# Attention and GEGLU FFN on one core: a hand-written interleaved order, values as stationary operand, and q and k turned by transposing DMAs

## The chip, the core and the metric

The kernel runs on one NeuronCore of a Trainium2 chip. The metric is the device time of one execution in microseconds (us). The core has five engines that work side by side, each with its own instruction queue: TensorE (PE; its weight loads are listed apart as PEld), VectorE (DVE), ScalarE (ACT), GpSimd (POOL) and SyncE (SP). Instructions of one engine are issued in the order of its queue. Transfers run on DMA engines; POOL and SP issue them.

## What is computed

Eight batches with eight heads go through causal attention with a window of 128 positions and a distance bias; the result feeds a gated FFN.

```python
# q, k, v: [8, 8, 576, 64]
scores = scale * q @ k.T                                   # scale = 1/8
rel = pos[:, None] - pos[None, :]
mask = (rel >= 0) & (rel < 128)
scores = where(mask, scores - slope[h] * abs(rel), -1e9)   # slope[h] = 2**-(h+1)
attn = exp(scores - max); attn = attn / (sum(attn) + 1e-9)
x = (attn @ v) -> [4608 tokens, 512]
out = (gelu(x @ w_gate) * (x @ w_val)) @ w_out             # 512 -> 1536 -> 512
```

## The kernel before

Data is bf16 on chip, sums are float32 in PSUM. A batch has 576 positions, that is five tiles of 128 keys (the last of 64). Work is written as two functions, `attention_bp` for a pair of batches and `ffn_group` for 512 tokens, called in the order: pair 0, groups 0 and 1, pair 1, groups 2 and 3, pair 2, groups 4 and 5, pair 3, groups 6 to 8. No order of the engines' queues is written out; the framework's scheduler places the instructions by their dependences, and pools of buffers limit how far it runs ahead.

*Attention of a pair.* q, k and v are loaded from POOL with a cast to bf16, five DMAs each for a batch (`qsb`, `ksb`, `vsb`; L113, L132). q and k must stand with the head dimension on partitions: TensorE transposes each in four chunks of two heads (five transposes a chunk, L98), and the results are copied out of PSUM by ScalarE and VectorE in turn (`evac`, L90 and L92) into `qT` and `kT`. For each head and key tile, one matmul for each of the two batches gives the scores (L158; the keys are the stationary operand, 64 partitions of head dimension, up to 256 queries are streamed). ScalarE takes the exponent (L164) and VectorE multiplies by the mask with the bias, `emask` (L168). For the product with v the probabilities `pT` are the stationary operand and v with an appended column of ones is streamed (`vp`, 65 columns, L185): nine short matmuls for a batch and head. The 65th column of the result is the row sum. VectorE takes its reciprocal, five values a partition (L192, L193), and multiplies (L195, L201) into `xnat`, which has tokens on partitions. TensorE transposes `xnat` (L98 again) into `xT`, features on partitions, as the FFN needs it.

*FFN group.* For each of 12 slices of the hidden size, four matmuls with `wg` and four with `wv` (L222, L231), 512 tokens each, a gelu on ScalarE (L227), and a product on VectorE into `hT` (L235). Then four token tiles of 12 matmuls with `wo` (L240), copied out in turn by ScalarE and VectorE (L90, L92) and stored by SP (L246).

PSUM is split into pools: three banks for scores and transposes (`sc`), two for value products (`opp`), two for gate and value (`gv`), one for the output (`po`).

Of the kernel before, what the change touches and what calls it, by code (L numbers as in the profile page):

```python
# [10 lines left out]
ALU = mybir.AluOpType  # L12


@with_exitstack
def kernel(
# [10 lines left out]
    nc = tc.nc  # L27
# [5 lines left out]
    NKT = (S + 127) // 128  # L33
    LAST = S - 128 * (NKT - 1)

    consts = ctx.enter_context(tc.tile_pool(name="consts", bufs=1))
    slab_pool = ctx.enter_context(tc.tile_pool(name="slabs", bufs=2))
    qkT_pool = ctx.enter_context(tc.tile_pool(name="qkT", bufs=3))
    v_pool = ctx.enter_context(tc.tile_pool(name="vp", bufs=3))
    pT_pool = ctx.enter_context(tc.tile_pool(name="pT", bufs=3))  # L40
    xnat_pool = ctx.enter_context(tc.tile_pool(name="xnat", bufs=2))
    r_pool = ctx.enter_context(tc.tile_pool(name="rp", bufs=4))
    ffn_sb = ctx.enter_context(tc.tile_pool(name="ffn_sb", bufs=3))
    out_sb_pool = ctx.enter_context(tc.tile_pool(name="out_sb", bufs=3))
    ps_sc = ctx.enter_context(tc.tile_pool(name="ps_sc", bufs=3, space=bass.MemoryType.PSUM))
    ps_o = ctx.enter_context(tc.tile_pool(name="ps_o", bufs=2, space=bass.MemoryType.PSUM))
    ps_gv = ctx.enter_context(tc.tile_pool(name="ps_gv", bufs=2, space=bass.MemoryType.PSUM))
    ps_out = ctx.enter_context(tc.tile_pool(name="ps_out", bufs=1, space=bass.MemoryType.PSUM))

    ident = consts.tile([128, 128], BF16)  # L50
    nc.gpsimd.memset(ident, 0.0)
    nc.gpsimd.affine_select(
        out=ident, in_=ident, compare_op=ALU.not_equal, fill=1.0,
        base=0, pattern=[[-1, 128]], channel_multiplier=1,
    )

    emask = consts.tile([128, H, 256], BF16)
    init_pool = tc.alloc_tile_pool(name="init", bufs=1)
    relt = init_pool.tile([128, 256], mybir.dt.int32)
    tmpl = init_pool.tile([128, 256], FP32)  # L60
    nc.gpsimd.iota(relt, pattern=[[1, 256]], base=0, channel_multiplier=-1)
    nc.gpsimd.tensor_copy(out=tmpl, in_=relt)
    nc.gpsimd.affine_select(
        out=tmpl, in_=tmpl, compare_op=ALU.is_ge, fill=1e9,
        base=0, pattern=[[1, 256]], channel_multiplier=-1,
    )
    nc.gpsimd.affine_select(
        out=tmpl, in_=tmpl, compare_op=ALU.is_ge, fill=1e9,
        base=W - 1, pattern=[[-1, 256]], channel_multiplier=1,
    )  # L70
# [3 lines left out]
    init_pool.release()  # L74

    wg = consts.tile([128, 4, DFF], BF16)
    wv = consts.tile([128, 4, DFF], BF16)
    wo = consts.tile([128, 12, DM], BF16)

    xT = consts.tile([128, 4, NTOK], BF16)  # L80

    qspan = [(128 * j, min(256, S - 128 * j)) for j in range(NKT)]
    pslot = [256 * j for j in range(NKT)]
    PTW = 256 * (NKT - 1) + LAST

    evac_flip = [0]

    def evac(dst, src):
        if evac_flip[0] % 2 == 0:
            nc.scalar.copy(out=dst, in_=src)  # L90
        else:
            nc.vector.tensor_copy(out=dst, in_=src)  # L92
        evac_flip[0] += 1

    def pe_transpose_block(ps_bf16, src):
        for j in range(NKT):
            sz = 128 if j < NKT - 1 else LAST
            nc.tensor.transpose(  # L98
                out=ps_bf16[:, 128 * j:128 * j + sz],
                in_=src(j, sz),  # L100
                identity=ident[0:sz, 0:sz],
            )

    def attention_bp(bp):
        bb = (2 * bp, 2 * bp + 1)
        qT, kT, vnat, xnat = {}, {}, {}, {}
        for b in bb:
            qsb = slab_pool.tile([128, NKT, DM], BF16, name="qsb")
            ksb = slab_pool.tile([128, NKT, DM], BF16, name="ksb")
            for sb, src in ((qsb, q), (ksb, k)):  # L110
                for j in range(NKT):
                    sz = 128 if j < NKT - 1 else LAST
                    nc.gpsimd.dma_start(  # L113
                        out=sb[0:sz, j, :].rearrange("p (h d) -> p h d", h=H),
                        in_=src[b][:, 128 * j:128 * j + sz, :].rearrange(
                            "h p d -> p h d"),
                    )

            qT[b] = qkT_pool.tile([128, 4, S], BF16, name="qT")
            kT[b] = qkT_pool.tile([128, 4, S], BF16, name="kT")  # L120
            for sb, dst in ((qsb, qT[b]), (ksb, kT[b])):
                for c in range(4):
                    pst = ps_sc.tile([128, 512], FP32, name="sc")
                    pstb = pst.bitcast(BF16)
                    pe_transpose_block(
                        pstb, lambda j, sz: sb[0:sz, j, 128 * c:128 * (c + 1)])
                    evac(dst[:, c, :], pstb[:, 0:S])

            vsb = slab_pool.tile([128, NKT, DM], BF16, name="vsb")
            for j in range(NKT):  # L130
                sz = 128 if j < NKT - 1 else LAST
                nc.gpsimd.dma_start(  # L132
                    out=vsb[0:sz, j, :].rearrange("p (h d) -> p h d", h=H),
                    in_=v[b][:, 128 * j:128 * j + sz, :].rearrange(
                        "h p d -> p h d"),
                )
            vnat[b] = v_pool.tile([128, NKT, H, 65], BF16, name="vp")
            nc.vector.memset(vnat[b][:, :, :, 64:65], 1.0)  # L138
            nc.vector.tensor_copy(
                out=vnat[b][:, 0:NKT - 1, :, 0:64],  # L140
                in_=vsb[:, 0:NKT - 1, :].rearrange("p j (h d) -> p j h d", h=H),
            )
            nc.vector.tensor_copy(
                out=vnat[b][0:LAST, NKT - 1, :, 0:64],
                in_=vsb[0:LAST, NKT - 1, :].rearrange("p (h d) -> p h d", h=H),
            )
            xnat[b] = xnat_pool.tile([128, NKT, DM], BF16, name="xnat")

        for h in range(H):
            hc, hp = h // 2, (h % 2) * 64  # L150
            pT = pT_pool.tile([128, 2, PTW], BF16)
            for j in range(NKT):
                kp = 128 if j < NKT - 1 else LAST
                q0, nq = qspan[j]
                sc = ps_sc.tile([128, 512], FP32, name="sc").rearrange(
                    "p (x n) -> p x n", x=2)
                for i, b in enumerate(bb):
                    nc.tensor.matmul(  # L158
                        out=sc[0:kp, i, 0:nq],
                        lhsT=kT[b][hp:hp + 64, hc, 128 * j:128 * j + kp],  # L160
                        rhs=qT[b][hp:hp + 64, hc, q0:q0 + nq],
                        start=True, stop=True,
                    )
                nc.scalar.activation(  # L164
                    out=pT[0:kp, :, pslot[j]:pslot[j] + nq],
                    in_=sc[0:kp, :, 0:nq], func=AF.Exp, scale=0.125,
                )
                nc.vector.tensor_tensor(  # L168
                    out=pT[0:kp, :, pslot[j]:pslot[j] + nq],
                    in0=pT[0:kp, :, pslot[j]:pslot[j] + nq],  # L170
                    in1=emask[0:kp, h:h + 1, 0:nq].to_broadcast((kp, 2, nq)),
                    op=ALU.mult,
                )

            for i, b in enumerate(bb):
                opp = ps_o.tile([128, NKT, 65], FP32, name="opp")
                for qt in range(NKT):
                    qs = 128 if qt < NKT - 1 else LAST
                    mms = []
                    if qt > 0:  # L180
                        mms.append((qt - 1, pslot[qt - 1] + 128))
                    mms.append((qt, pslot[qt]))
                    for mi, (j, col) in enumerate(mms):
                        kp = 128 if j < NKT - 1 else LAST
                        nc.tensor.matmul(  # L185
                            out=opp[0:qs, qt, :],
                            lhsT=pT[0:kp, i, col:col + qs],
                            rhs=vnat[b][0:kp, j, h, :],
                            start=(mi == 0), stop=(mi == len(mms) - 1),
                        )  # L190
                r = r_pool.tile([128, NKT], FP32)
                nc.vector.reciprocal(r[:, 0:NKT - 1], opp[:, 0:NKT - 1, 64])  # L192
                nc.vector.reciprocal(  # L193
                    r[0:LAST, NKT - 1:NKT], opp[0:LAST, NKT - 1, 64:65])
                nc.vector.tensor_tensor(  # L195
                    out=xnat[b][:, 0:NKT - 1, 64 * h:64 * h + 64],
                    in0=opp[:, 0:NKT - 1, 0:64],
# [91 lines left out]
```

## Time and profile before

| what | value |
|---|---|
| median of 3 runs | 528.34 us (527.97 to 529.66) |
| span of the profiled execution, first to last instruction | 527.3 us |
| TensorE busy | 487.2 us, 92% |
| VectorE busy | 205.2 us, 39% |
| ScalarE busy | 188.4 us, 36% |
| POOL busy | 105.7 us, 20% |
| mean granted TensorE clock | 0.880 |

The profiled execution's span lies about 1 us below the median of the runs: the span leaves out what stands ahead of the first and behind the last instruction. In a group's row, the names are output<-input, then the shapes (partitions x elements), the count, the busy time, the mean in ns of one, and the idle time just before such instructions with what ended it. Matmuls are pipelined, so the length of one is longer than the distance between two starts. In a row of stretches, the first numbers are the limits and the length, then the busy time of PE, PEld, DVE, ACT and POOL with counts, the granted clock, the DMA share and GB/s.

### The profile page before, as it was taken

What the parts mean: (1) busy time and instruction counts of PE and PEld (TensorE: products, weight loads), DVE (VectorE), ACT (ScalarE), POOL (GpSimd) and SP (SyncE); (2) the same over time, 40 slices, a digit from 0 to 9 for tenths busy, and PEclk for the clock granted to TensorE, in tenths of its full rate; (3) what the DMA queues carried; (4) which work ended last, traced back from release to release, by engine and by line L of the source; (5) the groups of instructions that cost most, each with busy time, mean ns of one, the idle gap of its engine ahead of it and who ended that gap; (6) DMA issues with size and microseconds to landing.
All of it is one profiled execution on the core that took longest, in us unless ns stands there. A gap on an engine that the chain in (4) does not pass through costs nothing.

```text
span 527.3 us, 6826 instructions
## 1 busy us (share of the span) xinstructions
PE 487.2 (92%) x2638; PEld 239.9 (45%) x2672; DVE 205.2 (39%) x614; ACT 188.4 (36%) x350; POOL 105.7 (20%) x133
## 2 busy tenths in 40 slices
PE   3499899999989899999899999999899899999995
PEld 1255554444555544444555544444455434444432
DVE  0255644333354653142345643232354633232331
ACT  3166243132365243122565152132565232132220
POOL 9961796300440030002720000000000000000000
PEclk9999999999955589999955599999855589999999
DMA  9999999910990070102990000101100000201102
GB/s 88 138 178 210 158 142 101 106 40 2 125 90 1 0 47 0 61 20 31 167 63 2 0 1 1 73 8 41 42 0 1 0 1 0 81 1 41 40 0 81
DMA packets 120336, 28.76 MB, mean 55 GB/s; under 512 B 113136, under 2 KB 114672, under 8 KB 120304
## 3 DMA queue, kind: packets, MB, share of 16 engines
q0 software_dynamic: 115120, 18.88, 47.2%
q1 hardware_dynamic: 5184, 9.44, 4.7%
q8 instruction: 21, 0.34, 0.3%
q14 instruction: 11, 0.09, 0.0%
HBM read 37.75 MB, written 9.44 MB: 89 GB/s over the span
## 4 chain that ended last, share of the span: by engine, by line
PE 80%; DMA 6%; POOL 5%; ACT 4%; DVE 3%; issue 1%; another core or an unknown queue 1%; DVEq 0%; POOLq 0%; ACTq 0%
PE gv L231 20%; PE gv L222 17%; PE po L240 17%; PE opp L185 10%; PE sc L158 8%; PE sc L98 7%; DMA wv<-in_moe_w_val_dram 4%; DMA ksb<-in_k_dram 2%; POOL ksb L113 2%; POOL vsb L132 2%; POOL qsb L113 1%; ACT pT L164 1%; DVE hT L235 1%; ACT L164 1%
## 5 line engine op out<-in xcount | busy, mean ns | idle before, releaser
L235 DVE TENSOR_TENSOR hT<-gv,gelu 128x512 bf16<-128x512 f32 x108 | 74.7, 692 | 116.3 <-PE gv L231 111.9
L222 PE MATMUL gv<-xT,wg 128*128 128x512 bf16 x419 | 112.9, 388 | 2.4 <-ACT gelu L227 2.0
L231 PE MATMUL gv<-xT,wv 128*128 128x512 bf16 x420 | 112.6, 385 | 2.3 <-DVE hT L235 1.0
L227 ACT ACTIVATE gelu<-gv 128x512 bf16<-128x512 f32 x108 | 64.5, 597 | 133.5 <-PE gv L222 124.4
L240 PE MATMUL po<-wo,hT 128*128 128x512 bf16 x423 | 98.5, 379 | 2.7 <-ACT osb L90 1.3
L164 ACT ACTIVATE pT<-sc 128x512 bf16<-128x512 f32 (+2 forms) x160 | 71.2, 513 | 44.0 <-PE sc L158 27.5
L158 PE MATMUL sc<-qT,kT 64*128 64x256 bf16 (+2 forms) x320 | 75.0, 354 | 6.1 <-ACT pT L164 5.2
L185 PE MATMUL opp<-vp,pT 128*128 128x65 bf16 (+2 forms) x576 | 75.6, 246 | 4.3 <-DVE xnat L201 4.1
L231 PEld LDWEIGHTS <-wv 128*128 128x128 bf16 x432 | 42.4, 98 | 65.7 <-issue 27.5
L185 PEld LDWEIGHTS <-pT 128*128 128x128 bf16 (+2 forms) x576 | 46.9, 122 | 42.3 <-issue 11.8
L222 PEld LDWEIGHTS <-wg 128*128 128x128 bf16 x432 | 42.0, 98 | 52.3 <-issue 3.6
L240 PEld LDWEIGHTS <-hT 128*128 128x128 bf16 x432 | 41.8, 98 | 52.0 <-issue 4.0
L168 DVE TENSOR_TENSOR pT<-pT,emask 128x512 bf16<-128x512 bf16 (+2 forms) x160 | 48.5, 359 | 6.1 <-ACT pT L164 5.6
L113 POOL DMA_DIRECT2D qsb<-in_q_dram x40 | 34.4, 897 | 59.3 <-PE sc L98 59.1
L113 POOL DMA_DIRECT2D ksb<-in_k_dram x40 | 33.8, 888 | 54.4 <-PE sc L98 35.7
L92 DVE COPY osb<-po 128x512 f32<-128x512 f32 x18 | 12.5, 692 | 80.4 <-PE po L240 75.1
L132 POOL DMA_DIRECT2D vsb<-in_v_dram x40 | 34.0, 895 | 47.2 <-DVE vp L138 38.6
L158 PEld LDWEIGHTS <-kT 64*128 64x128 bf16 (+1 forms) x320 | 31.2, 122 | 26.0 <-issue 10.2
L192 DVE RECIPROCAL r<-opp 128x4 f32<-128x4 f32 x64 | 10.8, 176 | 61.5 <-PE opp L185 61.0
L90 ACT COPY osb<-po 128x512 f32<-128x512 f32 x18 | 10.5, 585 | 67.5 <-PE po L240 64.5
L98 PE MATMUL sc<-ident,qsb 128*128 128x128 bf16 (+1 forms) x160 | 19.2, 242 | 14.5 <-DMA qsb<-in_q_dram 13.2
L90 ACT COPY xT<-sc 128x576 bf16<-128x576 bf16 x16 | 10.2, 638 | 46.3 <-PE sc L98 46.3
(33 smaller groups left out, 198.4 us busy)
## 6 DMA issues: line engine op xcount, KB each, us to landing
out_dram<-osb SPq DMA_DIRECT2D x36, 256.0 KB, 2.0
qsb<-in_q_dram POOLq DMA_DIRECT2D x32, 128.0 KB, 4.4
ksb<-in_k_dram POOLq DMA_DIRECT2D x32, 128.0 KB, 4.9
vsb<-in_v_dram POOLq DMA_DIRECT2D x32, 128.0 KB, 4.1
wg<-in_moe_w_gate_dram POOLq DMA_DIRECT2D x1, 1536.0 KB, 12.1
wv<-in_moe_w_val_dram POOLq DMA_DIRECT2D x1, 1536.0 KB, 18.7
wo<-in_moe_w_out_dram POOLq DMA_DIRECT2D x1, 1536.0 KB, 25.6
qsb<-in_q_dram POOLq DMA_DIRECT2D x8, 64.0 KB, 4.0
```

The costliest lines, as they stand in the source:

```text
L98: nc.tensor.transpose(out=ps_bf16[:, 128 * j:128 * j + sz], in_=src(j, sz), identity=ident[0:sz, 0:sz],)
L113: nc.gpsimd.dma_start(out=sb[0:sz, j, :].rearrange("p (h d) -> p h d", h=H), in_=src[b][:, 128 * j:128 * j + sz, :].rearrange("h p d -> p ...
L132: nc.gpsimd.dma_start(out=vsb[0:sz, j, :].rearrange("p (h d) -> p h d", h=H), in_=v[b][:, 128 * j:128 * j + sz, :].rearrange("h p d -> p h ...
L158: nc.tensor.matmul(out=sc[0:kp, i, 0:nq], lhsT=kT[b][hp:hp + 64, hc, 128 * j:128 * j + kp], rhs=qT[b][hp:hp + 64, hc, q0:q0 + nq], start=T ...
L164: nc.scalar.activation(out=pT[0:kp, :, pslot[j]:pslot[j] + nq], in_=sc[0:kp, :, 0:nq], func=AF.Exp, scale=0.125,)
L168: nc.vector.tensor_tensor(out=pT[0:kp, :, pslot[j]:pslot[j] + nq], in0=pT[0:kp, :, pslot[j]:pslot[j] + nq], in1=emask[0:kp, h:h + 1, 0:nq] ...
L185: nc.tensor.matmul(out=opp[0:qs, qt, :], lhsT=pT[0:kp, i, col:col + qs], rhs=vnat[b][0:kp, j, h, :], start=(mi == 0), stop=(mi == len(mms) ...
L222: nc.tensor.matmul(out=pg, lhsT=wg[:, c, 128 * f:128 * (f + 1)], rhs=xT[:, c, t0:t0 + 512], start=(c == 0), stop=(c == 3),)
L227: nc.scalar.activation(out=gelu, in_=pg, func=AF.Gelu)
L231: nc.tensor.matmul(out=pv, lhsT=wv[:, c, 128 * f:128 * (f + 1)], rhs=xT[:, c, t0:t0 + 512], start=(c == 0), stop=(c == 3),)
L235: nc.vector.tensor_tensor(out=hT[:, f, :], in0=pv, in1=gelu, op=ALU.mult)
L240: nc.tensor.matmul(out=po, lhsT=hT[:, f, 128 * t:128 * (t + 1)], rhs=wo[:, f, :], start=(f == 0), stop=(f == 11),)
```

## The change

The kernel is rewritten with a manual order: on each engine the instructions stand as the program writes them. The unit is now one batch b and one FFN group g = b - 1. Batch 0 is done first, alone. Then for each group: its 12 gate/value slices, and after them the attention of batch g + 1 with the group's output matmuls, cut into eight halves of six matmuls (`out_half`), set between its parts. Groups 7 and 8 have no attention beside them.

- A chunk c is two heads. Scores of its two heads are issued alternately (i = 0, 1; partitions 0 to 63 and 64 to 127) into two banks. Key tiles are shifted by 64 positions, so that tile 0 holds 64 zero keys and 64 real ones, and queries are streamed 192, 256, 256, 256 and 128 at a time. Masks are applied to both heads at once, 1024 and 1152 elements a partition (`emask`, and `emask2`, a second arrangement of it).
- In `values`, v (64 columns of a head) is the stationary operand and the probabilities are streamed, so that the product comes out with features on partitions, the form of `xT`; the two heads go to the two halves of the output partitions. The row sums come from the same matmuls with `ones` in place of v. Reciprocals and products run on those shapes: 320 and 256 columns, on 128 partitions. `xnat` and its transposes are gone.
- q and k of batch 0 are still transposed by TensorE. For batches 1 to 7, ten transposing DMAs a batch, issued on SP (`transposes_dma`), write `kT` and `qT` from the loaded slabs.
- v is loaded straight into its place (`vb`), wg and wv come in four column slices each, and all PSUM use takes its bank from one pool of eight.

```diff
+    ctx.enter_context(tc.manual_schedule(
+        engines={ENG.PE, ENG.Activation, ENG.DVE, ENG.Pool, ENG.SP}))
...
+    def transposes_dma(b):
+        for nm, dst, off in (("ksb", kT[b % 2], 64), ("qsb", qT[b % 2], 0)):
+            for j in range(5):
+                sz = min(128, S - 128 * j)
+                nc.sync.dma_start_transpose(
+                    out=dst[:, :, off + 128 * j:off + 128 * j + sz],
+                    in_=slabs[nm, b][0:sz, j, :])
...
+    def score(b, c, i, j, ps, col):
+        lo = 64 * i
+        nc.tensor.matmul(
+            out=ps[:, col:col + NQ[j]],
+            lhsT=kT[b % 2][lo:lo + 64, c, 128 * j:128 * j + 128],
+            rhs=qT[b % 2][lo:lo + 64, c, Q0[j]:Q0[j] + NQ[j]],
+            start=True, stop=True)
...
+    def scores1(b, c):
+        P = probs[b, c - c % 2][:, c % 2]
+        ps = [bank(), bank()]
+        for j in (1, 2):
+            for i in (0, 1):
+                score(b, c, i, j, ps[i], PCOL[j])
+        for i in (0, 1):
+            exp(P[:, i, 0:512], ps[i])
+        mask(P[:, :, 0:512].rearrange("p i (n x) -> p i n x", n=2),
+             emask[:, 2 * c:2 * c + 2, :].unsqueeze(2).to_broadcast((128, 2, 2, 256)))
...
+    def values(b, c):
+        P = probs[b, c - c % 2][:, c % 2]
+        x, y, z = bank(), bank(), bank()
+        for what in (0, 1):
+            for j in range(5):
+                for (a, e, ps, base) in (
+                        (Q0[j], min(Q0[j] + NQ[j], QS), (x, z)[what], 0),
+                        (max(Q0[j], QS), Q0[j] + NQ[j], y, 256 * what - QS)):
...
+                    for i in (0, 1):
+                        col = PCOL[j] + a - Q0[j]
+                        w = (vb[b % 2][:, j, 64 * (2 * c + i):64 * (2 * c + i) + 64]
+                             if what == 0 else ones)
+                        nc.tensor.matmul(
+                            out=ps[64 * i:64 * i + 64, base + a:base + e],
+                            lhsT=w, rhs=P[:, i, col:col + e - a],
+                            start=first, stop=last, skip_group_check=True)
+        r = r_pool.tile([128, S], FP32, name="r")
+        t0 = b * S
+        nc.vector.reciprocal(r[:, 0:QS], z[:, 0:QS])
+        nc.vector.tensor_tensor(out=xT[:, c, t0:t0 + QS], in0=x[:, 0:QS],
+                                in1=r[:, 0:QS], op=ALU.mult)
+        nc.vector.reciprocal(r[:, QS:S], y[:, 256:512])
+        nc.vector.tensor_tensor(out=xT[:, c, t0 + QS:t0 + S], in0=y[:, 0:256],
+                                in1=r[:, QS:S], op=ALU.mult)
...
+    load_qk(0)
+    nc.vector.memset(ident, 0.0)
+    nc.gpsimd.affine_select(
...
+    for g in range(NG):
+        b = g + 1
+        if 1 < b < B:
+            load_qk(b)
+            load_v(b)
+        for f in range(NF):
+            gate_val(g, f)
+            if b < B and f == 0:
+                transposes_dma(b)
+        if b < B:
+            scores0(b, 0)
+            scores1(b, 0)
+            out_half(g, 0)
+            scores2(b, 0)
+            out_half(g, 1)
+            scores1(b, 1)
+            out_half(g, 2)
+            scores2(b, 1)
+            values(b, 0)
+            out_half(g, 3)
+            scores0(b, 2)
+            scores1(b, 2)
+            out_half(g, 4)
+            scores2(b, 2)
+            values(b, 1)
+            scores1(b, 3)
+            out_half(g, 5)
+            scores2(b, 3)
+            values(b, 2)
+            out_half(g, 6)
+            values(b, 3)
+            out_half(g, 7)
```

`scores0` does key tile 4 of two chunks, `scores2` key tiles 0 and 3 of one; their exps are 256 and 448 columns long.

VectorE's queue within attention, before (two heads' worth; `pT` probabilities, `opp` the value product, `r` the reciprocal; numbers are buffers):

```order
L201 TENSOR_TENSOR xnat_1398<-opp_1552,r_1562 64x64
L168 TENSOR_TENSOR pT_1567<-pT_1567,emask_99 128x2x256 x2
L168 TENSOR_TENSOR pT_1567<-pT_1567,emask_99 128x2x192
L168 TENSOR_TENSOR pT_1567<-pT_1567,emask_99 64x2x64
L168 TENSOR_TENSOR pT_1623<-pT_1623,emask_99 128x2x256
L192 RECIPROCAL r_1603<-opp_1593 128x4
L193 RECIPROCAL r_1603<-opp_1593 64x1
L192 RECIPROCAL r_1618<-opp_1608 128x4
L195 TENSOR_TENSOR xnat_1317<-opp_1593,r_1603 128x4x64
L201 TENSOR_TENSOR xnat_1317<-opp_1593,r_1603 64x64
L193 RECIPROCAL r_1618<-opp_1608 64x1
```

The same queue now, at the end of a batch's attention and the beginning of the next group's gate/value block (`P` probabilities, `ps` PSUM banks):

```order
L145 TENSOR_TENSOR P_719<-P_719,emask_87 128x2x512
L105 COPY osb_800<-ps_737 128x512
L145 TENSOR_TENSOR P_719<-P_719,emask2_88 128x2x576
L203 RECIPROCAL r_839<-ps_814 128x320
L204 TENSOR_TENSOR xT_84<-ps_812,r_839 128x320
L206 RECIPROCAL r_839<-ps_813 128x256
L207 TENSOR_TENSOR xT_84<-ps_813,r_839 128x256
L203 RECIPROCAL r_878<-ps_853 128x320
L204 TENSOR_TENSOR xT_84<-ps_851,r_878 128x320
L206 RECIPROCAL r_878<-ps_852 128x256
L207 TENSOR_TENSOR xT_84<-ps_852,r_878 128x256
L224 TENSOR_TENSOR hT_909<-ps_911,gelu_920 128x512
```

Reciprocals have grown from 1 and 4 elements a partition to 256 and 320, and the last two chunks' stand one behind the other ahead of the first `hT` of the next group.

SP's queue, as a difference (lines with - are before, with + now): the stores of a group now have the next batch's transposes ahead of them.

```order
-L246 DMA out_dram<-osb 128x512 x36
-L284 UNCONDITIONAL_BRANCH
+L351 UNCONDITIONAL_BRANCH
+L127 DMA_TRANSPOSE kT_92<-ksb 128x4x128 x4
+L127 DMA_TRANSPOSE kT_92<-ksb 128x4x64
+L127 DMA_TRANSPOSE qT_90<-qsb 128x4x128 x4
+L127 DMA_TRANSPOSE qT_90<-qsb 128x4x64
+L241 DMA out_dram<-osb 128x512 x4
```

Ten transposes of batch 1 stand first, then the four stores of group 0; so it goes on for every group up to 6, and the last twelve stores stand alone.

POOL's queue at the start, now: the pieces of q and k come ahead of the small operations that make the identity and the mask.

```order
L81 DMA qsb<-in_q_dram 128x8x64 x4
L81 DMA qsb<-in_q_dram 64x8x64
L81 DMA ksb<-in_k_dram 128x8x64 x4
L81 DMA ksb<-in_k_dram 64x8x64
L246 ISA
L246 AFFINE_SELECT ident<-ident 128x128
L251 IOTA relt 128x256
L252 CAST tmpl<-relt 128x256
L254 AFFINE_SELECT tmpl<-tmpl 128x256 x2
```

Before, the identity's select and the mask's small operations stood ahead of or between the first three loads; now all ten loads of batch 0 are issued first.

More of the change, by code (lines that the diff above doesn't have):

```diff
@@ new lines @@
+    values(0, 3)
+    for g in range(NG):
[30 more added lines that the diff above has]
+            out_half(g, 7)
+        else:
+            for u in range(8):
+                out_half(g, u)
```

356 lines of the change are left out of this document (158 added, 198 removed).

## The prediction

> **What bounds the kernel now.** I read the head of the page first, then stretches of the span, the chain, the groups by form, and a few microseconds of timeline.
>
> ```profile
> span 527.3 us, 6826 instructions
> PE 487.2 (92%) x2638; PEld 239.9 (45%) x2672; DVE 205.2 (39%) x614; ACT 188.4 (36%) x350; POOL 105.7 (20%) x133
> PEclk9999999999955589999955599999855589999999
> ```
>
> TensorE is busy 92% and its granted clock falls three times. The stretches below are cut at the attention phases (columns: length, then each engine's busy time; the clock follows POOL).
>
> ```profile
> 0.00:75.00 75.00, 56.33 (x369) 31.65 (x371) 32.33 (x129) 31.40 (x65) 54.88 (x73) 1.00 1.76 153
> 144.50:188.50 44.00, 40.76 (x270) 23.30 (x270) 24.39 (x110) 21.64 (x46) 6.53 (x8) 0.53 0.43 28
> 188.50:260.50 72.00, 71.07 (x357) 32.67 (x365) 24.24 (x42) 22.93 (x38) 14.33 (x17) 1.00 0.47 54
> 421.00:527.30 106.30, 97.69 (x416) 41.58 (x423) 29.06 (x42) 26.11 (x43) 0.00 (x0) 0.98 0.08 30
> 61.73 1.59 PE opp L185 x15
> 178.84 1.59 PE opp L185 x15
> 211.47 2.59 PE po L240 x12
> ```
>
> Attention of two batches takes 44 us at about half clock. The first phase reads 1.00, but its run of 15 value products takes the same 1.59 us as the run in the half-clock phase, so I read it as slow too. Two FFN groups with the next loads take 72. At full clock a 512-column matmul costs 2.59/12 = 0.216 us. A group has 96 gate/value matmuls and 48 output matmuls: 20.7 and 10.4 us, 31.1 together, nine groups 280. So about 247 us of the span is attention and stalls. That part can be won.
>
> **The parts and their costs.** The durations:
>
> ```profile
> L235 DVE TENSOR_TENSOR hT<-gv,gelu 128x512 bf16<-128x512 f32 x108 | 74.7, 692 | 116.3 <-PE gv L231 111.9 <-PE gv L222 2.4 <-ACT gelu L227 2.0
> L164 ACT ACTIVATE pT<-sc 128x512 bf16<-128x512 f32 x96 | 52.5, 597 | 41.6 <-PE sc L158 25.8 <-PE opp L185 14.3 <-DVE xnat L201 0.3
> L168 DVE TENSOR_TENSOR pT<-pT,emask 128x512 bf16<-128x512 bf16 x96 | 37.2, 412 | 6.1 <-ACT pT L164 5.6
> L168 DVE TENSOR_TENSOR pT<-pT,emask 128x384 bf16<-128x384 bf16 x32 | 11.1, 346 | 0.0
> L195 DVE TENSOR_TENSOR xnat<-opp,r 128x256 bf16<-128x256 f32 x64 | 25.6, 399 | 0.0
> L201 DVE TENSOR_TENSOR xnat<-opp,r 64x64 bf16<-64x64 f32 x64 | 13.2, 206 | 0.0
> L192 DVE RECIPROCAL r<-opp 128x4 f32<-128x4 f32 x64 | 10.8, 176 | 61.5 <-PE opp L185 61.0
> L193 DVE RECIPROCAL r<-opp 64x1 f32<-64x1 f32 x64 | 8.9, 139 | 0.0
> L92 DVE COPY osb<-po 128x512 f32<-128x512 f32 x18 | 12.5, 692 | 80.4 <-PE po L240 75.1 <-remote 5.3
> L98 PE MATMUL sc<-ident,qsb 128*128 128x128 bf16 x128 | 16.1, 250 | 14.5 <-DMA qsb<-in_q_dram 13.2 <-DVE qT L92 1.0
> L98 PE MATMUL sc<-ident,xnat 128*128 128x128 bf16 x128 | 20.0, 291 | 1.0 <-DVE xnat L201 0.7 <-DMA ksb<-in_k_dram 0.2
> L227 ACT ACT_TABLE_LOAD x4 | 5.1, 1283 | 0.6 <-PE sc L98 0.6
> 34.32 0.18 DVE L192 RECIPROCAL r<-opp 128x4 f32<-128x4 f32 x1 [1.34 <-PE opp L185]
> 34.42 0.13 DVE L193 RECIPROCAL r<-opp 64x1 f32<-64x1 f32 x1
> 34.48 0.15 DVE L192 RECIPROCAL r<-opp 128x4 f32<-128x4 f32 x1
> 34.56 0.41 DVE L195 TENSOR_TENSOR xnat<-opp,r 128x256 bf16<-128x256 f32 x1
> 34.88 0.21 DVE L201 TENSOR_TENSOR xnat<-opp,r 64x64 bf16<-64x64 f32 x1
> 35.01 0.15 DVE L193 RECIPROCAL r<-opp 64x1 f32<-64x1 f32 x1
> 34.09 0.24 PE L158 MATMUL sc<-qT,kT 64*64 64x64 bf16 x1
> 34.10 0.24 PE L185 MATMUL opp<-vp,pT 64*64 64x65 bf16 x1
> ```
>
> *TensorE.* Gone are 280 of 320 transposes of q and k and all 160 of the attention output. Scores keep their 320 matmuls with 8704 columns a batch, now in pairs on upper and lower partitions. Values become 96 matmuls a batch, 17408 columns, in pairs on the two halves of the output partitions. The last two rows show matmuls on different parts of the array starting 0.01 us apart, so I take pairs as running together: at 0.216/512 us a column, (8704 + 17408)/2 columns are 5.5 us a batch; singly they would be 11. With the 10.4 of output matmuls and about 20 changes of shape at some 0.1 us (an estimate), a section of attention has 18 us of TensorE work.
>
> *ScalarE.* Eight exps of 512 (0.60), eight of 448 (about 0.55), four of 256 (about 0.40), two copies and two table loads (1.28 each): 14.5 us a section, beside the others.
>
> *VectorE.* Masks: 66 ns for 128 more elements gives 0.68 us for 1024 and 0.74 for 1152; four of each, 5.7. Products by 1/sum: (399-206)/192 = 1.0 ns an element, so 0.46 for 320 and 0.40 for 256; four pairs, 3.4. Two evacuations, 1.4. The **reciprocals** change most: from 5 values a head and batch to 576 values for a pair of heads, 320 and 256 at a time. No such size is in the trace. In the timeline three more elements cost 0.02 us (0.15 against 0.13) and 0.03 (0.18 against 0.15), 6.7 and 10 ns an element; by the group means 37/3 = 12.3. If a reciprocal went like the product, it would be 1.0. The ends are 1.0 and 12.3; I take 8.5, amid the like pairs of the timeline: 0.14 + 319 x 0.0085 = 2.85 us, and 2.31 for 256. Four chunks a batch are 20.6 us. VectorE's section is 31.1 us of work against TensorE's 18: VectorE becomes the bound there. Over the run, one ns an element is 8 x 2304 = 18.4 us.
>
> [...]
>
> *One period.* FFN group g needs batch g's four chunks, so VectorE's queue and the next gate/value block are one chain. From the block's last matmul to the first reciprocal: a table load 1.3 and ten exps some 0.47 apart, begun about 1.5 before that matmul ends, then a mask 0.7: 5.2 us. Then up to the first product of the fourth chunk: three chunks of 6.0 (2.85+0.46+2.31+0.40), 3.3 of the fourth, four masks 2.8, an evacuation 0.7; less 0.9 because neighbours overlap (0.41 long, the next starts 0.32 later), plus 1.5 of waits for TensorE: 25.4, say 25.5. Groups 1 and 2 need also the second product, 2.7 more. TensorE then has waited over 5 us, and its clock may have fallen. The stretch from 421 has a clock of 0.98: about 4 us at half speed (0.02 x 106.3/0.5), a loss of 2. The price is 0 to 4, two such dips; I take 4, since here TensorE stands idle first. Period: 20.7 + 5.2 + 25.5 + 4 = 55.4, for two of the seven 58.1. Seven: 393.
>
> *Transposing DMAs.* Ten on SP for each batch 1 to 7, behind the previous group's output stores.
>
> ```profile
> ksb<-in_k_dram POOLq DMA_DIRECT2D x32, 128.0 KB, 4.9
> out_dram<-osb SPq DMA_DIRECT2D x36, 256.0 KB, 2.0
> wo<-in_moe_w_out_dram POOLq DMA_DIRECT2D x1, 1536.0 KB, 25.6
> 62.74 4.24 POOL L113 DMA_DIRECT2D qsb<-in_q_dram  x5
> L73 ACT ACTIVATE emask<-tmpl 128x256 bf16<-128x256 f32 x8 | 2.6, 402 | 2.6 <-POOL tmpl L67 2.6
> L139 DVE COPY vp<-vsb 128x2048 bf16<-128x2048 bf16 x8 | 6.4, 801 | 1.6 <-DMA vsb<-in_v_dram 1.6
> 523.41 0.69 DVE L92 COPY osb<-po 128x512 f32<-128x512 f32 x1 [6.32 <-PE po L240]
> 524.13 0.33 SPq L246 DMA_DIRECT2D out_dram<-osb  x1
> 504.56 1.03 PE L222 MATMUL gv<-xT,wg 128*128 128x512 bf16 x4
> 506.44 1.03 PE L222 MATMUL gv<-xT,wg 128*128 128x512 bf16 x4
> ```
>
> A 128 KB piece of k takes 0.85 us of issue (4.24/5) and 4.9 to land. Ten pieces therefore cost 8.5 us if they stream, 49 if each waits for the one before. Their cover is the gate/value block with its cold start, 24.7, and less 2 for the landing, 22 to 24. I take 1 to 2 us each, near the streaming row since nothing makes one wait for the last, and cost them at nothing; the cover is gone at about 2.4 us each.
>
> *Beginning, end, FFN.* The identity's select now stands behind ten POOL issues: 0.7 + 8.5 + 1.9 of small work, then the mask exps 2.6 and VectorE's copies of the second mask about 2 (0.80 for the largest): evacuations start near 16, the first reciprocal near 23. Batch 0's four chunks (24), two more evacuations, four masks and waits bring the first gate matmul to 52 (before, two batches were done by 75). Weights follow v of batch 0 and are covered: the last of the three matrices landed 25.6 us after its issue. Groups 7 and 8 have no attention: 2 x 31.1; the 1.88 us period of a gate/value pair (506.44-504.56) loses its 0.15 us stall since eight banks rotate. The tail stays at 3.2 after the last evacuation starts plus its 0.7, 4.
>
> Sum: 52 + 393 + 62.2 + 4 = 511 of span. To it I add some 30 handovers from engine to engine a period at 0.04 us (an estimate: the store at 524.13 starts 0.03 after the copy of 523.41 ends), 1.2 a period, 8 in all: 519. The median of the runs, 528.34, stands 1.0 over the profiled span, so **520**. Fast and slow of 0.3% (1.6 us) are about what can be told from no change.
>
> **Rivals.**
>
> *Reciprocals are cheap (0.20).* At 1 ns an element VectorE's section is 13.9 us and TensorE bounds: period 20.7 + 18 + 2.5 of waits = 41.2, start 35, so 35 + 288 + 62 + 4 = 389. Against it stand the four timeline rows; for it, that all of them are tiny. Intermediate slopes fill the room up to 500.
>
> *The transposes are late (0.17): slower.* At a landing of 4.9 us in series the ten take 49 us, 25 over the cover; seven times, 175: 695. At 3 us each, 6 over, 42: 562. It turns the forecast into a loss from 2.5 us each. Nothing in the trace shows one. [...]
>
> *TensorE stays at half clock and pairs do not overlap (0.08): slower.* Then a section is 2 x (10.4 + 11) + 2 = 45 us against VectorE's 31 to 35; seven times 10 to 14: 590 to 620. For it: attention never had full clock before. Against: runs of six dense matmuls between.
>
> **Chances.** Forecast 0.55, with its own range 495 to 550 (slopes 7.5 to 10): 0.34 faster, 0.05 same, 0.16 slower. Cheap reciprocals 0.20, faster. Late transposes 0.17 and slow TensorE 0.08, slower but for 0.01 and 0.01. Together faster 0.54, same 0.07, slower 0.39. The range, 430 to 585, leaves out the cheapest reciprocals (0.11) and the latest transposes and TensorE (0.09).
>
> **What would show it.** Right: a RECIPROCAL of 320 near 2.8 us and the costliest VectorE group, near 160 us with its smaller sister; gate matmuls waiting for xT at each group's start, 5 us and more; two batches' attention costing no separate 44 us; a clock that dips once a period. Wrong: a reciprocal under 1 us; score matmuls waiting for transposing DMAs; pairs starting a full stream apart.

## The result, and the profile after

The changed kernel takes 460.28 us (median of 4 runs, 459.21 to 461.51), the kernel before 528.15 us beside it (4 runs, 527.34 to 529.66): a ratio of 0.871 with a 95% interval of 0.869 to 0.874, 13% faster. The forecast was 520 us. The profiled execution spans 457.4 us.

The head of the page after, and its line on the chain that ended last, by engine (the chain is followed back from the last instruction, at each step to what that step waited for):

```profile
span 457.4 us, 6209 instructions
PE 377.6 (83%) x2424; PEld 179.0 (39%) x2424; DVE 283.7 (62%) x332; ACT 173.0 (38%) x314; POOL 110.3 (24%) x138
PEclk9996799869997899889997999899989998899999
...
PE 54%; DVE 38%; ACT 3%; POOL 2%; issue 2%; POOLq 0%
```

TensorE lost 110 us of busy time, VectorE gained 78.5, and the chain now runs over both: 54% TensorE, 38% VectorE. The groups by form show where VectorE's time is:

```profile
L203 DVE RECIPROCAL r<-ps 128x320 f32<-128x320 f32 x32 | 68.8, 2150 | 0.0
L206 DVE RECIPROCAL r<-ps 128x256 f32<-128x256 f32 x32 | 55.9, 1747 | 0.0
L204 DVE TENSOR_TENSOR xT<-ps,r 128x320 bf16<-128x320 f32 x32 | 15.7, 491 | 1.1
```

64 columns more cost 2150 - 1747 = 403 ns: 6.3 ns an element; the line through these two widths has 134 ns at no columns. The two reciprocals are 124.7 us, 15.6 a batch.

What TensorE waits for, the longest three rows of the waits (us in total, times, longest):

```profile
PE ps L197 <- DVE P L145: 32.4, 9, 4.2
PE ps L219 <- DVE xT L207: 13.0, 4, 4.1
PE ps L219 <- DVE xT L204: 10.8, 5, 2.8
```

The last two are gate matmuls that wait for a batch's last chunks. The first are value products that wait for a mask; that mask had waited in VectorE's queue behind a reciprocal (in the chain, a reciprocal of 256 columns from 235.57 to 237.25 and the mask at 237.62). No wait for a transposing DMA is among them. VectorE's first reciprocal and the last product of batch 0 in the timeline, and one period in the chain (start, length, what; pieces under 0.36 us are left out):

```profile
23.69 2.15 DVE L203 RECIPROCAL r<-ps 128x320 f32<-128x320 f32 x1
47.86 0.43 DVE L207 TENSOR_TENSOR xT<-ps,r 128x256 bf16<-128x256 f32 x1
```

```profile
199.40 20.23 PE ps L219 x93
219.63 0.44 PE ps L135 x8
220.07 1.40 PE ps L234 x6
221.77 1.40 PE ps L234 x6
223.49 1.40 PE ps L234 x6
225.31 0.36 issue
225.67 0.55 ACT P L142
226.24 0.76 DVE P L145
227.00 2.08 DVE r L203
...
244.28 2.07 DVE r L203
246.38 0.50 DVE xT L204
246.92 20.23 PE ps L219 x93
```

From 227.00 to 246.9 the chain is on VectorE alone: reciprocals, products, masks, one evacuation, and 0.3 us without a visible cause. Then the gate/value block follows. A period is 246.92 - 199.40 = 47.5 us.

### The profile page after: what moved, and what is told of

Read it like the earlier page. It is cut to its first block, busy times and chain, and to the rows that moved or that the text cites. A ratio compares the mean times of both kernels' runs of the same rounds, so it can differ in the third digit from the quotient of the medians.

```text
span 457.4 us, 6209 instructions
## 1 busy us (share of the span) xinstructions
PE 377.6 (83%) x2424; PEld 179.0 (39%) x2424; DVE 283.7 (62%) x332; ACT 173.0 (38%) x314; POOL 110.3 (24%) x138
## 4 chain that ended last, share of the span: by engine, by line
PE 54%; DVE 38%; ACT 3%; POOL 2%; issue 2%; POOLq 0%
PE ps L219 41%; DVE r L203 15%; PE ps L234 11%; DVE r L206 10%; DVE P L145 6%; DVE xT L204 3%; ACT P L142 3%; PE ps L135 2%; DVE xT L207 2%; POOL qsb L81 1%; DVE osb L105 1%; POOL ksb L81 1%; ACT emask L264 1%; DVE qT L105 0%; DVE emask L267 0%
## 5 line engine op out<-in xcount | busy, mean ns | idle before, releaser
L224 DVE TENSOR_TENSOR hT<-ps,gelu 128x512 bf16<-128x512 f32 x108 | 74.7, 692 | 112.4 <-PE ps L219 105.3
L219 PE MATMUL ps<-xT,wg 128*128 128x512 bf16 x432 | 117.8, 393 | 23.8 <-DVE xT L207 13.0
L219 PE MATMUL ps<-xT,wv 128*128 128x512 bf16 x432 | 114.4, 388 | 0.0
L234 PE MATMUL ps<-wo,hT 128*128 128x512 bf16 x432 | 109.9, 398 | 1.7 <-ACT osb L107 1.7
L223 ACT ACTIVATE gelu<-ps 128x512 bf16<-128x512 f32 x108 | 64.0, 597 | 120.9 <-PE ps L219 120.8
L142 ACT ACTIVATE P<-ps 128x512 bf16<-128x512 f32 (+2 forms) x160 | 73.7, 542 | 21.6 <-PE ps L135 21.6
L219 PEld LDWEIGHTS <-wv 128*128 128x128 bf16 x432 | 42.9, 99 | 76.9 <-issue 28.3
L203 DVE RECIPROCAL r<-ps 128x320 f32<-128x320 f32 x32 | 68.8, 2150 | 0.0
L145 DVE TENSOR_TENSOR P<-P,emask 128x1024 bf16<-128x1024 bf16 x64 | 45.5, 721 | 26.2 <-ACT P L142 26.1
L90 POOL DMA_DIRECT2D vb<-in_v_dram x40 | 34.1, 869 | 92.9 <-PE ps L197 92.1
L206 DVE RECIPROCAL r<-ps 128x256 f32<-128x256 f32 x32 | 55.9, 1747 | 0.0
L81 POOL DMA_DIRECT2D ksb<-in_k_dram x40 | 33.8, 887 | 17.1 <-DMA wo<-in_moe_w_out_dram 10.2
```

Source lines behind the costliest of these rows:

```text
L81: nc.gpsimd.dma_start(out=t[0:sz, j, :].rearrange("p (h d) -> p h d", h=H), in_=src[b][:, 128 * j:128 * j + sz, :].rearrange("h p d -> p h ...
L90: nc.gpsimd.dma_start(out=t[lo:128, j, :].rearrange("p (h d) -> p h d", h=H), in_=v[b][:, 128 * j - 64 + lo:128 * j + 64, :].rearrange("h ...
L142: nc.scalar.activation(out=dst, in_=src, func=AF.Exp, scale=0.125)
L145: nc.vector.tensor_tensor(out=dst, in0=dst, in1=m, op=ALU.mult)
L203: nc.vector.reciprocal(r[:, 0:QS], z[:, 0:QS])
L206: nc.vector.reciprocal(r[:, QS:S], y[:, 256:512])
```

## Experiments

Two numbers stand for each: the time with its ratio to the kernel before, and the late period, the distance in the trace between the fifth gate/value weight loads of groups 4 and 5 (the first of a block that cannot run until the batch is done).

| kernel | us | ratio to before (95%) | late period, us |
|---|---|---|---|
| changed kernel | 460.28 | 0.871 (0.869 to 0.874) | 47.5 |
| reciprocals are copies | 390.42 | 0.738 (0.736 to 0.740) | 38.9 |
| reciprocals on ScalarE | 389.92 | 0.738 (0.736 to 0.740) | 39.0 |
| reciprocals twice | 589.92 | 1.115 (1.111 to 1.118) | 63.0 |
| output halves first | 535.17 | 1.012 (1.009 to 1.015) | 58.3 |
| transposes on TensorE | 484.20 | 0.914 (0.911 to 0.918) | 51.0 |
| transposing DMAs left out | 459.96 | 0.869 (0.866 to 0.872) | 47.5 |
| matmuls in TensorE's gaps | 460.85 | 0.870 (0.868 to 0.873) | 47.5 |
| probabilities stationary | 412.97 | 0.780 (0.777 to 0.784) | 41.9 |
| ScalarE, q and k of batch 1 earlier | 388.37 | 0.733 (0.731 to 0.736) | 39.0 |
| the same, output weights earlier | 384.79 | 0.727 (0.724 to 0.730) | 39.0 |

**Theory A:** VectorE's chain of reciprocals sets the length of each attention section; TensorE's work there is done in its shadow. **Theory B:** TensorE's work, or its clock, sets it.

### Reciprocals replaced by copies

```diff
-        nc.vector.reciprocal(r[:, 0:QS], z[:, 0:QS])
+        nc.vector.tensor_copy(out=r[:, 0:QS], in_=z[:, 0:QS])
...
-        nc.vector.reciprocal(r[:, QS:S], y[:, 256:512])
+        nc.vector.tensor_copy(out=r[:, QS:S], in_=y[:, 256:512])
```

> The reciprocals of 320 and 256 columns are replaced by plain copies of the same shapes (the division of the attention is left out). Theory A, VectorE's chain of reciprocals is the bound of each attention section: a copy of 512 f32 from PSUM took 0.69 us, so 320 and 256 should take about 0.45 and 0.38 in place of 2.15 and 1.75, 3.1 us less a chunk and 12.3 a batch. TensorE's work of the section then bounds (about 18 us with its output matmuls, against 27 from the last gate matmul to the next first one now), so a period of 48 falls to 41 to 43 and batch 0 by 8 to 12: 395 to 420 us in place of 460. Theory B, the reciprocals lie beside TensorE's work and TensorE or its clock bounds: less than 10 us change, 450 to 460.

Measured 390.42 us, 70 less, and somewhat below the range that I expected. Two groups, and the chain by engine:

```profile
L203 DVE COPY r<-ps 128x320 f32<-128x320 f32 x32 | 15.4, 482 | 0.0
L206 DVE COPY r<-ps 128x256 f32<-128x256 f32 x32 | 13.2, 413 | 0.0
...
PE 76%; DMA 8%; POOL 5%; SPq 4%; DVE 4%; issue 2%; ACT 1%; POOLq 0%
```

VectorE lost 96 us of work (a copy of the same shape takes 482 ns where the reciprocal took 2150), the kernel 70; VectorE left the chain (4%). Theory B is out. The 26 us that did not come back are where TensorE became the bound: the period stops at 38.9, of which TensorE is busy for 38.2 (205.40 to 244.30).

### Reciprocals made twice

```diff
         nc.vector.reciprocal(r[:, 0:QS], z[:, 0:QS])
+        nc.vector.reciprocal(r[:, 0:QS], z[:, 0:QS])
...
         nc.vector.reciprocal(r[:, QS:S], y[:, 256:512])
+        nc.vector.reciprocal(r[:, QS:S], y[:, 256:512])
```

> Each reciprocal is made twice (the second time over the first): 15.6 us more of VectorE work a batch. Theory A, VectorE's chain of reciprocals sets the length of each attention section: all of it is seen, eight batches, +120 to +130 us: 578 to 590 us. If a part of the reciprocals lies beside work that would set the length anyway, less: under 570 us. TensorE bounds: under 480 us.

Measured 589.92 us, 129.6 more. The added groups and the chain:

```profile
L204 DVE RECIPROCAL r<-ps 128x320 f32<-128x320 f32 x32 | 69.0, 2157 | 1.1
L208 DVE RECIPROCAL r<-ps 128x256 f32<-128x256 f32 x32 | 56.2, 1757 | 1.1
...
DVE 49%; PE 44%; ACT 2%; POOL 2%; issue 2%; POOLq 0%
```

69.0 + 56.2 = 125.2 us of work were added, and 129.6 us of time. Not all of that is the reciprocals themselves: the gate/value blocks of groups 0 to 7 are 12 us longer in the chain (179.6 against 167.5 us together), with a mean granted clock of 0.823 against 0.933. The other 118 us are nearly the whole of the added work, so the reciprocals are nearly all on the path.

### The order undone: output halves first

```diff
         if b < B:
+            for u in range(8):           # written out in the kernel
+                out_half(g, u)
             scores0(b, 0)
             scores1(b, 0)
-            out_half(g, 0)
             scores2(b, 0)
-            out_half(g, 1)
...
```

> The interleave undone: all eight halves of a group's output matmuls stand ahead of the next batch's attention, everything else as it is. Theory A, VectorE's chain bounds the section and the output matmuls are done in its shadow: of their 10.4 us a group nearly all, less some 2 us that ScalarE's first exps overlap with, comes onto the path, 8 to 10 us a period, eight periods: 520 to 540 us, and the granted clock falls more often since the attention has no dense matmuls in it. Theory B, TensorE's total work bounds and its order does not matter: 455 to 470.

Measured 535.17 us, 75 more. The chain of one period:

```profile
193.21 0.86 PE ps L234 x4
194.12 9.46 PE ps L234 x43
203.60 0.59 ACT osb L107
204.21 1.28 ACT L142
205.50 4.38 ACT P L142 x10
209.90 0.76 DVE P L145
210.66 2.08 DVE r L203
```

The output matmuls (10.4 us) now stand in the chain, and ScalarE's table load and ten exps follow one after another: 17.5 us from the last gate matmul to the first reciprocal, against 7.4. The interleave is worth 75 us, more than the whole 68 that the change won; without it the kernel is 1.2% slower than before. The mean granted clock was 0.862 against 0.933 in the profiled executions.

### The DMA transposes undone, and left out

```diff
-            if b < B and f == 0:
-                transposes_dma(b)
+            if b < B and f >= 4:
+                transposes(b, f - 4)
```

> The transposing DMAs of batches 1 to 7 undone: q and k are transposed by TensorE, eight times five transposes a batch, one set behind each of the last eight gate/value slices, and copied out by VectorE and ScalarE in turn as for batch 0. Theory A as it stands says that TensorE bounds the gate/value block: 40 transposes at some 0.06 to 0.12 us on TensorE are 2.5 to 5 us a period, seven periods: 477 to 495 us. Rival, the transposing DMAs delay something now (stores or loads), and taking them out pays for a part of that: 460 to 470.

Measured 484.20 us, 24 more. Two neighbouring slices of a gate/value block in the chain:

```profile
175.31 1.83 PE ps L219 x8
177.50 1.83 PE ps L219 x8
```

A slice takes 1.83 us and the next starts 2.19 after it: 0.36 us for five transposes between them. Eight slices are 2.9 us of the 3.5 by which a period grew (51.0 against 47.5); the rest was not taken apart.

The other kernel issues no transposes for batches 2 to 7 (`if b < 2 and f == 0`).

> The transposing DMAs of batches 2 to 7 are left out (those batches use the q and k that were turned for an earlier one). Theory A, they are hidden behind the gate/value block: no change, 457 to 463 us. Rival, their 13 us on SP or their traffic delay the output stores, the loads or the scores: faster by 1 us or more a period, 435 to 453 us.

Measured 459.96 us: no change. In the changed kernel the transposing DMAs of batches 2 to 7 cost nothing that the times can tell. SP's queue, and the median landing times (the last figure, us):

```profile
95.65 7.45 SPq L127 DMA_TRANSPOSE kT<-ksb  x5
103.16 6.48 SPq L127 DMA_TRANSPOSE qT<-qsb  x5
...
kT<-ksb SPq DMA_TRANSPOSE x35, 3.2
qT<-qsb SPq DMA_TRANSPOSE x35, 2.4
```

Ten take 14 us of SP, 1.3 to 1.5 each, and land in 2.4 to 3.2. That is less than the 22 to 24 us of cover.

### Matmuls set into the gaps of TensorE

```diff
+            keep_warm(12)                # 512-column matmuls nobody reads
             values(b, 3)
             out_half(g, 7)
+            keep_warm(10)
```

> The clock priced: 22 matmuls of 512 columns whose result nobody reads are set into the two gaps of TensorE in each period, 12 ahead of the fourth chunk's value products (gap 3.8 us) and 10 behind the last output half (gap 3.5 us); at full speed they take 2.6 and 2.2 us. If the clock falls because of these gaps, the granted clock rises from 0.93 towards 0.98 and the gate/value block falls from 21.7 to 20.5 us, the fourth chunk's value products a little too: 445 to 455 us. By the price in the prediction (4 us a period): 428 to 436 us. If the dips have another cause, or the added matmuls do not fit into the gaps: 460 to 475 us.

Measured 460.85 us (6 runs, 457.82 to 461.17): no change; of the three expectations the last came in, and the first, which I held to, was wrong. The clock did rise, to a mean of 0.976 against 0.933 in the profiled executions:

```profile
PEclk9996799989999899999999999999999999999999
...
199.79 20.23 PE ps L219 x93
```

But the gate/value block of these later groups takes 20.23 us here and took 20.23 in the changed kernel: there the low clock lay in the stretch in which TensorE waits for VectorE anyway (0.62 from 193.00 to 199.40). Of the changed kernel's blocks with attention ahead of them only those of groups 0, 1, 2 and 7 were slower, 21.55 to 21.73 us; group 2's row in its chain:

```profile
150.39 21.73 PE ps L219 x93
```

By the PEclk rows the clock dips here at the blocks of groups 0 to 2 as there, and only the dip at group 7's is gone, whose block was 1.4 us longer than 20.23 there: the times cannot tell that. The granted clock (the number after POOL's) tells the slow blocks from the others; the first two rows are the beginnings of the blocks of groups 2 and 3 in the changed kernel, the last two the same with the added matmuls:

```profile
150.39:157.00 6.61, 6.61 (x24) 2.72 (x24) 1.70 (x3) 3.07 (x4) 0.00 (x0) 0.77 0.40 90
199.40:206.00 6.60, 6.60 (x31) 3.03 (x31) 4.18 (x6) 3.56 (x5) 0.00 (x0) 1.00 0.67 132
```

```profile
150.70:157.00 6.30, 6.30 (x22) 2.51 (x22) 1.38 (x2) 3.07 (x4) 0.00 (x0) 0.75 0.78 131
199.79:206.00 6.21, 6.21 (x29) 2.81 (x29) 4.11 (x5) 3.56 (x5) 0.00 (x0) 1.00 1.74 127
```

The slow blocks begin at 0.75 to 0.80 and then run at 1.00 (group 2's in the changed kernel from 154.00 to 172.00). Groups 0 to 2 need the second product of the fourth chunk too, so TensorE stands idle 3.5 to 4.1 us just before them in the changed kernel (4.13, 3.60, 3.54); the added matmuls did not shorten that (4.13, 4.09, 4.09), since no filler stands ahead of group 0 and those ahead of groups 1 and 2 are done before the wait ends. Group 3 waits 1.39 us there and 1.97 here. So in the changed kernel the blocks behind 3.54 to 4.13 us of idle time began at 0.77 to 0.80, those behind 1.33 and 1.39 us (groups 4 and 3) at 1.00, and behind 2.55 to 2.81 us both occur (groups 5 and 6 at 1.00, group 7 at 0.78); with the added matmuls group 2 began at 0.75 behind 4.09 us and group 3 at 1.00 behind 1.97. The price of the dips is some 1.5 us in a few blocks, not 4 in each. The gaps that matter most were not filled, so what a full filling would win is not shown; by these blocks it is at most some 6 us.

### Probabilities stationary again, in the new order

`values` is put back to the form before the change (tiles of 64 and 128 queries, a column of ones behind v), with 20 transposes a batch by TensorE; order and transposing DMAs stay.

```diff
+                    nc.tensor.matmul(
+                        out=opp[0:n, t, :], lhsT=P[:, i, col:col + n],
+                        rhs=vb[b % 2][:, j, h, :],
+                        start=(j == js[0]), stop=(j == js[-1]))
...
+            nc.vector.reciprocal(r[:, 1:5], opp[:, 1:5, 64])
+            nc.vector.reciprocal(r[0:64, 0:1], opp[0:64, 0, 64:65])
...
             out_half(g, 4)
+            x_transposes(b, 0)
```

> One part of the change undone: the order and the transposing DMAs stay, but the probabilities are the stationary operand again, as before the change (tiles of 64 and 128 queries, 65 columns streamed, the row sum in the 65th), with reciprocals of 4 and 1 elements, products into an array with tokens on partitions, and 20 transposes a batch by TensorE to the form of xT, each set of five behind the output half that follows its chunk. Theory A, the large reciprocals are what sets the section: they shrink from 15.6 us a batch to 8 x (0.18 + 0.14) = 2.5, VectorE's section falls to some 15 us, and TensorE's is 18.5 (the section in the kernel with reciprocals on ScalarE) less 8.5 of value products and row sums, plus 72 short matmuls at 0.06 to 0.106 us (the run of 15 in 1.59 us before the change) and 20 transposes at 0.07: 16 to 19. Period 38 to 42, whole 385 to 415 us: the new form of the value product lost what the order won. Rival, the short matmuls let the clock fall and TensorE needs about 28 us a section, as it needed 44 for two batches before: period 48 to 50, 460 to 485 us.

Measured 412.97 us, 47 less than the changed kernel. Two groups, the chain by engine, and TensorE's rows at a set of transposes:

```profile
L199 DVE RECIPROCAL r<-ps 128x4 f32<-128x4 f32 x64 | 11.0, 172 | 7.8 <-PE ps L194 7.8
L200 DVE RECIPROCAL r<-ps 64x1 f32<-64x1 f32 x64 | 8.3, 129 | 0.0
...
PE 69%; DMA 8%; DVE 7%; ACT 5%; POOL 4%; SPq 4%; issue 1%; POOLq 0%
...
216.30 0.53 PE L211 MATMUL ps<-ident,xnat 64*128 64x64 bf16 x5 [0.93 <-DVE xnat L204]
```

The reciprocals fall from 124.7 to 19.3 us, and VectorE's share of the chain from 38% to 7%. What remains over the 38.9 of the copies goes, by the chain, with TensorE's 20 transposes and the waits for `xnat`; it was not taken apart further. The short matmuls did not slow the clock (0.992). So everything in the change but the new form of the value product won 115 us (528 to 413), and that form gave 47 of them back, through its reciprocals: with these made on ScalarE (next section) the new form is 23 us faster than the old one.

### Reciprocals on ScalarE, and a shorter beginning

1/z is made as exp(-ln z) on ScalarE. One table set is loaded for both functions, once at the start and once ahead of each attention.

```diff
+    def shared_set():
+        nc.scalar.add_instruction(mybir.InstLoadActFuncSet(
+            name=nc.get_next_instruction_name(), act_func_set_id=6))
...
-        nc.vector.reciprocal(r[:, 0:QS], z[:, 0:QS])
+        nc.scalar.activation(out=r[:, 0:QS], in_=z[:, 0:QS], func=AF.Ln)
+        nc.scalar.activation(out=r[:, 0:QS], in_=r[:, 0:QS], func=AF.Exp, scale=-1.0)
...
         if b < B:
+            shared_set()
             scores0(b, 0)
```

> The whole computation, with each reciprocal taken off VectorE and made on ScalarE as exp(-ln(sum)), with a table that holds both functions loaded once at the start and once a period ahead of the attention's exps (as many table loads as before). Theory A, VectorE's chain bounds: VectorE loses 15.6 us a batch; ScalarE gains 16 instructions of 0.40 to 0.47 us a batch, about 7 us, and stands at some 21 us a section, beside TensorE's 18; a period falls from 48 to 43 to 46: 415 to 440 us. Theory B, TensorE bounds: no gain, and since the exps of the next scores queue behind the logarithms, somewhat slower: 460 to 475.

Measured 389.92 us, below what I expected and the same as with copies. ScalarE's groups, and the chain by engine:

```profile
L204 ACT ACTIVATE r<-r 128x320 f32<-128x320 f32 x32 | 15.0, 470 | 1.0
L203 ACT ACTIVATE r<-ps 128x320 f32<-128x320 f32 x32 | 14.3, 447 | 4.8 <-PE ps L197 4.8
...
PE 78%; DMA 7%; POOL 5%; SPq 4%; ACT 2%; issue 2%; DVE 0%; POOLq 0%
```

0.92 us on ScalarE in place of 2.15 on VectorE, and ScalarE had room: in a period of 38.9 us it is busy for 25.7, and TensorE now does 38.2 us of work. I had ScalarE as the next bound (43 to 46); its exps and logarithms fit beside TensorE. With one table set for both functions the trace has 16 table loads of 1.28 us, as many as in the changed kernel.

What is left is the beginning. TensorE's longest waits there in this kernel were 10.2 us for the identity that TensorE's transposes need, and the first row below; they led to the next kernel, whose new wait is the second row:

```profile
PE ps L135 <- DMA qT<-qsb: 9.2, 1, 9.2
```

```profile
PE ps L240 <- DMA wo<-in_moe_w_out_dram: 5.6, 1, 5.6
```

```diff
-    load_qk(0)
...
     nc.vector.memset(ident, 0.0)
     nc.gpsimd.affine_select(
...
+    load_qk(0)
...
         load_w(step * s, step * (s + 1))
-    load_qk(1)
+        if s == 1:
+            load_qk(1)
```

> The kernel with reciprocals on ScalarE (389.9 us), whose beginning is changed: the identity's select stands ahead of the loads of batch 0, and q and k of batch 1 are loaded between the second and the third slice of the weights instead of behind the fourth. In the former, TensorE waited 9.2 us for batch 1's last transposing DMA and 3.0 us for the first score operands. If these waits are what is left at the beginning, 9 to 12 us less: 378 to 382 us. If the later weights become the wait in their place: 385 to 392 us.

Measured 388.37 us: 1.5 less, not 9 to 12. In place of the wait for the identity stand waits for the pieces of q and k themselves (7.8 and 2.6 us). The wait for batch 1's transposes fell from 9.2 to 0.6 us, and the output weights, which had been covered by it, became late (5.6). Then these too:

```diff
+    for s in range(2):
+        nc.gpsimd.dma_start(
+            out=wo[:, 6 * s:6 * s + 6, :],
+            in_=moe_w_out[768 * s:768 * (s + 1), :].rearrange("(c p) f -> p c f", p=128))
     load_v(1)
-    nc.gpsimd.dma_start(out=wo, in_=moe_w_out.rearrange("(c p) f -> p c f", p=128))
```

> The kernel of e9_early_qk1 (388.4 us), in which TensorE waited 5.6 us for the output weights: these now come in two halves and ahead of v of batch 1. If that wait is the last one at the beginning that counts: 381 to 384 us. If v of batch 1 becomes late in its place, or the transfers just share what they have: 386 to 390 us.

Measured 384.79 us (6 runs, 382.99 to 385.64), just past the expected 381 to 384: the first period falls from 48.3 to 42.9 us, and this is the fastest kernel here, 27% under the time before.

## Why the prediction was wrong in size

The mechanism was the forecast one: VectorE's reciprocals set each attention section, gate matmuls wait for `xT`, the attention's separate 44 us a pair are gone, the transposing DMAs are hidden, pairs run together. The sum was 61.6 us too long (519 of span against 457.4). By its steps, one late period:

| step | predicted, us | measured, us | from |
|---|---|---|---|
| gate/value block | 20.7 | 20.2 | 199.40 to 219.63 |
| last gate matmul to first reciprocal | 5.2 | 7.4 | 219.63 to 227.00 |
| first reciprocal to first product of the fourth chunk | 25.5 | 19.9 | 227.00 to 246.92 |
| clock | 4 | 0; 1.5 in the first three | block 20.23, 21.73 |
| handovers | 1.2 | 0 | inside the rows above |
| sum | 56.6 | 47.5 | |

**The step that failed most: "I take 8.5, amid the like pairs of the timeline".** It measured 6.3 ns an element. In a period that is 4 x 0.77 + 3 x 0.63 = 5.0 us (2.85 against 2.08 and 2.31 against 1.68 in the chain), 35 us over seven. With the prediction's own 18.4 us for each ns, 2.2 ns are 40 us over all eight batches. What those 18.4 us assume, that every ns of reciprocal is seen, held nearly: doubling added 125.2 us of work and about as much time. The pairs of 1 and 4 elements, which differ by 20 to 40 ns in instructions of 130 to 180, could not carry a slope over 300 elements: if the same four rows are paired as VectorE's queue issues them for one result (0.18 with 0.13, 0.15 with 0.15), they give 16.7 and 0 ns. That the lower pair of the prediction, 6.7, lies near the 6.3 is luck.

**The clock term.** 4 us a period were charged, since TensorE stands idle before the block. It does, and the clock dips, but in four of seven periods the dip lies where VectorE sets the time (0.62 from 193.00 to 199.40, ahead of group 3) and the block runs at full speed. Seven times 4 less three times 1.5 is 23.5 us too much. The filling matmuls won nothing that the times can tell.

**Handovers.** 8 us added at the end were already in the durations of the stretches.

**The other way:** from the last gate matmul to the first reciprocal I counted a chain of exps. The chain shows another route: three output halves of 1.40 us stand in TensorE's queue between the scores, and VectorE's queue has the second chunk's last mask ahead of the first reciprocal. 2.2 us a period, 15 over seven.

Together: -35 for reciprocals, -4 for other work in that stretch, -23.5 clock, -8 handovers, -3 for the block, -1 for the second product in groups 1 and 2, +15 for the front: -59.5. The seven periods took 341.1 us against 401.

**The beginning** was near: first reciprocal at 23.69 (23 forecast), and the gate matmul that waits for the last product of batch 0 starts at 48.34 (52 forecast; the eight shorter reciprocals are 5.6 us, so something else took 2 us more). TensorE's section takes 18.3 us in the kernel with reciprocals on ScalarE (186.12 to 204.45 in its chain), nearly all of it busy; 18 was forecast. The 0.1 us for each of some 20 changes of shape, 2 of those 18 us, was my estimate, and no run shows it by itself: the output matmuls (10.4) and the paired columns (5.5) make 15.9 us, so 2.4 of the 18.3 went to all else.

**The rivals.** Cheap reciprocals: not so, but priced rightly: 389 us forecast, 390.4 with copies. Late transposes: ten take 14 us of SP's queue and land 2.4 to 3.2 us after their issue, the break would have been at 24. TensorE at half clock without pairs: not so; the 24 value matmuls of a chunk, 4352 columns, take 1.06 us (225.12 to 226.18), and one after another at 0.216 us for 512 columns they would take 1.84.

What the forecast left out, since it costed the parts only together: the interleave alone is worth 75 us, and the value product in its old form would have left the kernel at 413.

## What to carry to other kernels

Before a broadcast quantity is made wide (a row sum repeated over 64 partitions, so that its reciprocal has hundreds of columns), price the reciprocal at the width it will have (here 2150 ns for 320 columns, 176 for 4), and give a slope from tiny shapes a wide range. When work of one engine is moved into the shadow of another, look for the engine that casts the shadow: here ScalarE, 38% busy, could take it over, and 70 us were won. In this kernel a clock dip cost time only where it overlapped work on the chain (1.3 to 1.5 us in each of four blocks), so charge it by the stretch and not by the share.

## What the runs showed of the hardware that I had not expected

- A reciprocal from PSUM in f32 took 134 ns + 6.3 ns an element (2150 ns for 320, 1747 for 256), where a copy took 482 and 413. Two widths give this line; it meets the rows of one element (140 ns by the line, 139 and 129 measured) and lies under those of four (159 against 176 and 172).
- ln and exp on ScalarE took 447 + 470 ns for the same 320 columns; with one table set for both, the kernel had 16 table loads, as many as the changed kernel.
- Raising the mean granted clock from 0.933 to 0.976 won no time in this kernel (460.85 against 460.28 us).
- A gate/value block began at a granted clock of 0.75 to 0.80 behind 3.5 to 4.1 us of idle TensorE, and at 1.00 behind 1.3 to 2.0 us; behind 2.55 to 2.81 us two began at 1.00 and one at 0.78.
